# Attention block on one core: two query blocks start on the first 512 keys under a bound of their own, engines take turns on a PSUM bank, and the last output sums are held behind the last PV

## The chip, the cores and the metric

The kernel runs on one core of a Trainium2 chip. The metric is the device time of one execution in microseconds (us), the median of several runs. TensorE is called PE, VectorE DVE, ScalarE ACT, GpSimd POOL and SyncE SP. PSUM is where this kernel puts PE's products (tiles PA, PD and PO), in banks of 128 x 512 f32 values. "Span" is the time from the first to the last instruction of a profiled execution; it is some 1.8 us shorter than the time of the same run.

## The reference

```python
# x: 1 x 2048 x 448, wqkv: 448 x 1344, wo: 448 x 448, all bf16; H = 16 heads of 28
qkv = (x @ wqkv).reshape(B, S, 3, H, Dh).transpose(2, 0, 3, 1, 4)
q, k, v = qkv[0], qkv[1], qkv[2]
scores = jnp.einsum("bhqd,bhkd->bhqk", q, k) * (Dh ** -0.5)
p = softmax(scores, axis=-1)
o = jnp.einsum("bhqk,bhkd->bhqd", p, v)
out = o.transpose(0, 2, 1, 3).reshape(B, S, D) @ wo
```

## The kernel before

The 16 heads form four groups of four; a head is padded from 28 to 32 rows. A window is one group and one block of 512 queries; there are 16. In a window, each of 16 key tiles (128 keys) and four heads gives a score tile of 128 keys x 512 queries: 1024 tiles in all. Most tiles get their exponential on ACT, two at a time; the others go over DVE in three passes with a POOL product between them. PV products (exponentials times values) add a window's tiles up in one PSUM bank (PO).

```python
# two score tiles at once on ACT
nc.scalar.activation(out=PTA[pslot.idx][:, 0:len(ns) * QW], in_=PA[s.idx][:, 0:len(ns) * QW],
                     func=ACT.Exp, bias=ACT_BIAS, scale=ACT_SCALE)
# one score tile over DVE and POOL: p1, p2 (DVE), gq (POOL), f (DVE)
p1 = add(Op("DVE", P1, lambda: nc.vector.tensor_scalar(out=DU[b][:], in0=lo, ...)))
p2 = add(Op("DVE", P1, lambda: nc.vector.scalar_tensor_tensor(out=DV[b][:], in0=lo, ...)))
gq = add(Op("POOL", PTT, lambda: nc.gpsimd.tensor_tensor(out=DG[b][:], in0=DV[b][:], in1=DU[b][:], op=ALU.mult), ...))
f  = add(Op("DVE", P1, lambda: nc.vector.scalar_tensor_tensor(out=PTD[...], in0=PX[slot.idx][:], in1=DG[b][:], ...)))
```

The softmax subtracts a bound instead of the row's true maximum. The absolute values of a head's queries and its largest absolute keys, with a margin, are extra rows of the score product. The keys' maximum runs over all 2048 keys, so the first score of a group needs all four key blocks:

```python
# task_K: one of four key blocks of a group
red = add(Op("DVE", 0.61, lambda: nc.vector.tensor_reduce(
    out=KPART[g][:, sc:sc + 1], in_=ap(), axis=AX.X, op=ALU.max, apply_absolute_value=True), ...))
evs = [add(Op("ACT", 0.585, lambda pr=pr: nc.scalar.activation(      # waits for red; both read this bank
    out=KB[0][pr][:, cs], in_=ap(), func=ACT.Identity, bias=onescol[:, 0:1], scale=1.0), deps=[ops[-1], red], ...)) ...]
# task_kmax: over the four blocks, then written or broadcast into the keys' extra rows
m = add(Op("DVE", 0.12, lambda: nc.vector.tensor_reduce(out=KMAX[g][:], in_=KPART[g][:], axis=AX.X, op=ALU.max),
           deps=kmaxop[g], ...))
```

The order of the instructions on each engine is fixed when the kernel is built. The kernel lists operations with estimated durations, priorities and conditions, and a list scheduler in the kernel puts them in order; constants such as `QPR` or `UO` steer it. In the traces read here each engine works through its own list in that order: in the run below in which nine output sums stand ahead of the last PV products in PE's list, PE starts these sums at 402.07 us and those products at 403.88. In the last window, nine output products of the three earlier groups (`late_sums`, kind "A") may be placed before or after the last PV products; the final normalisation on DVE starts once PV has ended (in the trace of this kernel the last PV products start at 405.61 and take 0.39, DVE starts at 406.04):

```python
prev = add(Op("PE", 0.19, lambda: nc.tensor.matmul(out=PD[late_acc[tq]][:, 0:D],
    lhsT=OT[gg][NQC - 1][:, tq * P:(tq + 1) * P], rhs=WO[:, gg, :], start=(gg == 0), stop=False),
    prio=ACCP + tq + 0.1 * gg, kind="A", ...))
...
norm_dve(PO[:], DT[:], DR[:], ...)        # transpose, reciprocal, two transposes, two products, then four last matmuls
```

## Time and profile before

| | before |
|---|---|
| time, median of three runs (range) | 414.73 (414.67 to 415.01) |
| span of the profiled run | 413.1 |
| head: start to first exp | 16.38 |
| row: first exp to start of the last exp | 387.90, with 424 exps of 1024 columns |
| tail: start of the last exp to the end | 8.83 |

An "exp" is always one ACT instruction over two score tiles. A "step" is the time from the start of one to the start of the next; the steps were read from the starts in the trace. Their median is 0.916 us, and the mean of those without a hole is 0.9135. The kernel has six steps over 0.98; one is the second exp's (1.254), and four of the others are 1.17 to 1.19.

### The profile page before, as it was taken

The page shows a single profiled execution, that of the slowest core. Times are in us where ns is not written, and L with a number is a line of the kernel's source. Part 1 is how long each engine was busy: PE and PEld are TensorE (multiplying, and loading weights), DVE is VectorE, ACT ScalarE, POOL GpSimd, SP SyncE. Part 2 cuts the span into 40 slices and gives each one's busy share as a digit, 9 for nine tenths or more (in the row PEclk, how much of TensorE's full clock was granted, in tenths as well). Part 3 has the DMA queues.
Part 4 walks back from the last instruction along what each step waited for, and adds up shares of the span by engine and source line. Part 5 has one row for each costly group of instructions (what it writes and reads, how often), then busy time and mean ns, then how long its engine had stood idle before and what let it go on. Part 6 is the DMA issues. An engine that isn't in the chain of part 4 may idle for free.

```text
span 413.1 us, 7525 instructions
## 1 busy us (share of the span) xinstructions
PE 362.4 (88%) x2605; PEld 121.4 (29%) x2617; DVE 394.0 (95%) x696; ACT 400.0 (97%) x439; POOL 224.1 (54%) x203
## 2 busy tenths in 40 slices
PE   8988989898898889888898988979898888989995
PEld 4533232223232232322223222222322222222231
DVE  6899999999999999999999999999999999999975
ACT  4999999999999999999999999999999999999994
POOL 2155456464655556475465656547375656556450
PEclk9999999999999999999999999999999999999999
DMA  8410011202201001110400001010310101001012
GB/s 256 77 20 21 3 47 11 53 25 54 72 1 44 2 28 30 20 38 8 111 8 27 21 9 40 2 36 11 77 48 2 47 2 35 12 27 47 4 69 89
DMA packets 33413, 15.83 MB, mean 38 GB/s; under 512 B 26016, under 2 KB 30304, under 8 KB 33376
## 3 DMA queue, kind: packets, MB, share of 16 engines
q1 hardware_dynamic: 32304, 15.05, 14.5%
q8 instruction: 20, 0.33, 0.4%
q10 hardware_dynamic: 1072, 0.32, 0.3%
q14 instruction: 17, 0.14, 0.1%
HBM read 7.37 MB, written 1.96 MB: 23 GB/s over the span
## 4 chain that ended last, share of the span: by engine, by line
ACT 86%; issue 8%; PE 2%; DMA 2%; DVE 1%; SPq 0%; DVEq 0%; ACTq 0%
ACT PTA_131 L903 5%; ACT PTA_132 L903 4%; ACT PTA_133 L903 4%; ACT PTA_136 L903 4%; ACT PTA_135 L903 4%; ACT PTA_134 L903 4%; ACT PTA_145 L903 4%; ACT PTA_140 L903 4%; ACT PTA_139 L903 4%; ACT PTA_138 L903 4%; ACT PTA_137 L903 4%; ACT PTA_144 L903 4%; ACT PTA_142 L903 3%; ACT PTA_143 L903 3%; ACT PTA_141 L903 3%
## 5 line engine op out<-in xcount | busy, mean ns | idle before, releaser
L714 POOL TENSOR_TENSOR DG_181<-DV_175,DU_169 128x512 f16<-128x512 f16 x30 | 34.6, 1155 | 34.8 <-DVE DV_175 L711 34.6
L714 POOL TENSOR_TENSOR DG_182<-DV_176,DU_170 128x512 f16<-128x512 f16 x30 | 34.6, 1155 | 28.8 <-DVE DV_176 L711 28.7
L714 POOL TENSOR_TENSOR DG_184<-DV_178,DU_172 128x512 f16<-128x512 f16 x29 | 33.5, 1155 | 29.5 <-DVE DV_178 L711 28.2
L714 POOL TENSOR_TENSOR DG_186<-DV_180,DU_174 128x512 f16<-128x512 f16 x29 | 33.5, 1155 | 26.9 <-DVE DV_180 L711 26.7
L714 POOL TENSOR_TENSOR DG_185<-DV_179,DU_173 128x512 f16<-128x512 f16 x29 | 33.5, 1155 | 25.7 <-DVE DV_179 L711 25.6
L714 POOL TENSOR_TENSOR DG_183<-DV_177,DU_171 128x512 f16<-128x512 f16 x29 | 33.5, 1156 | 22.9 <-DVE DV_177 L711 22.7
L631 PEld LDWEIGHTS <-KB_1_94 64*128 64x128 bf16 x256 | 20.8, 92 | 48.4 <-issue 47.4
L631 PEld LDWEIGHTS <-KB_0_91 64*128 64x128 bf16 x256 | 20.5, 92 | 45.8 <-issue 42.1
L631 PEld LDWEIGHTS <-KB_1_92 64*128 64x128 bf16 x256 | 20.1, 93 | 45.8 <-issue 44.0
L631 PEld LDWEIGHTS <-KB_0_93 64*128 64x128 bf16 x256 | 20.3, 92 | 43.5 <-issue 42.5
L903 ACT ACTIVATE PTA_140<-PA_199 128x1024 bf16<-128x1024 f32 x18 | 22.4, 1247 | 0.0
L903 ACT ACTIVATE PTA_144<-PA_199 128x1024 bf16<-128x1024 f32 x18 | 22.4, 1245 | 0.0
L903 ACT ACTIVATE PTA_143<-PA_198 128x1024 bf16<-128x1024 f32 x18 | 22.3, 1241 | 0.0
L903 ACT ACTIVATE PTA_142<-PA_199 128x1024 bf16<-128x1024 f32 x18 | 22.3, 1239 | 0.0
L903 ACT ACTIVATE PTA_141<-PA_198 128x1024 bf16<-128x1024 f32 x18 | 22.3, 1236 | 0.0
L903 ACT ACTIVATE PTA_139<-PA_198 128x1024 bf16<-128x1024 f32 x17 | 21.1, 1241 | 0.0
L708 DVE TENSOR_SCALAR DU_171<-PD_202 128x512 f16<-128x512 uint16 x29 | 19.8, 682 | 1.0 <-PE PD_202 L631 0.7
L708 DVE TENSOR_SCALAR DU_172<-PD_200 128x512 f16<-128x512 uint16 x29 | 19.7, 681 | 0.9 <-PE PD_200 L631 0.9
L711 DVE SCALAR_TENSOR_TENSOR DV_178<-PD_200,DU_172 128x512 f16<-128x512 uint16 x29 | 19.8, 684 | 0.3
L711 DVE SCALAR_TENSOR_TENSOR DV_176<-PD_201,DU_170 128x512 f16<-128x512 uint16 x29 | 19.8, 683 | 0.2
L708 DVE TENSOR_SCALAR DU_169<-PD_200 128x512 f16<-128x512 uint16 x29 | 19.8, 682 | 0.2 <-PE PD_200 L631 0.2
L903 ACT ACTIVATE PTA_145<-PA_198 128x1024 bf16<-128x1024 f32 x16 | 20.0, 1247 | 0.0
(596 smaller groups left out, 1511.3 us busy)
## 6 DMA issues: line engine op xcount, KB each, us to landing
RRB_194<-SCR_196 SPq DMA_DIRECT2D x8, 256.0 KB
RRB_195<-SCR_197 SPq DMA_DIRECT2D x7, 256.0 KB
KB_1_94<-KB_0_93 SPq DMA_DIRECT2D x4, 128.0 KB
XS_127<-in_x_dram SPq DMA_DIRECT2D x1, 448.0 KB
XS_128<-in_x_dram SPq DMA_DIRECT2D x1, 448.0 KB
XS_129<-in_x_dram SPq DMA_DIRECT2D x1, 448.0 KB
XS_130<-in_x_dram SPq DMA_DIRECT2D x1, 448.0 KB
out_dram<-XS_127 SPq DMA_DIRECT2D x1, 448.0 KB
```

Source lines behind the costliest of these rows:

```text
L631: nc.tensor.matmul(out=ap, lhsT=KB[g % 2][i // 2][a:a + 64, j * P:(j + 1) * P], rhs=QB[w % NQB][i // 2][a:a + 64, :], start=True, stop=Tru ...
L708: p1 = add(Op("DVE", P1, lambda: nc.vector.tensor_scalar(out=DU[b][:], in0=lo, scalar1=SIG / 65536, scalar2=SIG * (SS - 0.5), op0=ALU.mult ...
L711: p2 = add(Op("DVE", P1, lambda: nc.vector.scalar_tensor_tensor(out=DV[b][:], in0=lo, scalar=65536 * (SS - 0.5 + CE / C3), in1=DU[b][:], o ...
L714: gq = add(Op("POOL", PTT, lambda: nc.gpsimd.tensor_tensor(out=DG[b][:], in0=DV[b][:], in1=DU[b][:], op=ALU.mult), deps=[p2], prio=n, kind ...
L903: nc.scalar.activation(out=PTA[pslot.idx][:, 0:len(ns) * QW], in_=PA[s.idx][:, 0:len(ns) * QW], func=ACT.Exp, bias=ACT_BIAS, scale=ACT_SCALE)
```

## The change

The intent is to start ACT's row earlier. Query blocks 0 and 1 of the first group take keys 0 to 511 (16 tiles each) under the maximum of these keys alone, which needs only the first block of x. Their partial PV sums are copied out of PO. Once the whole bound is known, a factor per query and head rescales them, and the rest of the block is added. Parts that go with it:

- the query weights are loaded second on the queue of the x blocks, and padded by ACT instead of POOL;
- the fourth block of x comes already transposed, by a DMA, not over PE and PSUM;
- reduce and copy of a key block's PSUM bank take turns as planned (in the kernel before, ACT's key copy waited twice for the reduce, 0.21 and 0.25 us), and DVE makes the copies of the second to fourth key block, which ACT made;
- the last output sums are held back while PV products are ready;
- many constants of the order are changed.

```diff
+    FB = TPC                # 4 key tiles = 512 keys
+    NF = 2                  # query blocks that start under their own bound
-    UO = 40
+    UO = 20
... (other constants cut)
     for b in range(NQC):
-        nc.sync.dma_start(out=XS[b][:], in_=x_perm[:, b * TPC:(b + 1) * TPC, :])
-    for (W, off) in ((WK, D), (WQ, 0)):
-        nc.scalar.dma_start(out=W[:, :, 0:GW], in_=wq3[:, :, off:off + GW])
+        if b < NQC - 1:
+            nc.sync.dma_start(out=XS[b][:], in_=x_perm[:, b * TPC:(b + 1) * TPC, :])
...
+        if b == 0:
+            nc.sync.dma_start(out=WQ[:, :, 0:GW], in_=wq3[:, :, 0:GW])
...
+    if XBAR:
+        for cc in range(CC):
+            nc.sync.dma_start(out=XT[NQC - 1][cc // 2][:, cc % 2, :],
+                              in_=bass.AP(x.tensor, x.offset + cc * CK, [[D, QW], [1, P]]), transpose=True)
...
+                evs[0].acq = lambda t: red.start is None or red.done(t)      # turns on one bank
+                red.acq = lambda t: evs[0].start is None or evs[0].done(t)
...
-                and kmrep[(g, j // TPC, i)].done(t))
+                and (w < NF and j < FB or kmrep[(g, j // TPC, i)].done(t)))
...
+    def task_factor(w):     # eight small matmuls, then
+        e = add(Op("ACT", 0.49, lambda: nc.scalar.activation(out=RRB[w][:], in_=bank(task)[:], func=ACT.Exp, scale=ACT_SCALE), ...))
+    def finish_block(w):
+        ev = add(Op("DVE", 0.62, lambda: nc.vector.tensor_copy(out=OSB[w][:], in_=PO[:]), ...))
+        first_part[w] = [add(Op("POOL", 1.22, lambda: nc.gpsimd.tensor_tensor(out=OSB[w][:], in0=OSB[w][:], in1=RRB[w][:], op=ALU.mult), ...))]
...
-        o = take_static(t, lambda o: o.kind == "A" and fits(o.dur, "F") or ...)
+        o = take_static(t, lambda o: o.kind == "A" and fits(o.dur, "F") and (pv_next[0] >= NROW or not pv_ready(pv_next[0], t)) or ...)
```

## The prediction

> **What bounds the kernel now.** I read the page first (busy shares, the 40 slices, the chain that ended last), then cut the span at the first and the last exp, then read both ends instruction by instruction.
>
> ```profile
> PE 362.4 (88%) x2605; PEld 121.4 (29%) x2617; DVE 394.0 (95%) x696; ACT 400.0 (97%) x439; POOL 224.1 (54%) x203
> ACT  4999999999999999999999999999999999999994
> ACT 86%; issue 8%; PE 2%; DMA 2%; DVE 1%; SPq 0%; DVEq 0%; ACTq 0%
> ```
>
> ACT is busy in every slice but the first and the last, and the chain runs along it for 86% of the span. The windows view (from:to, length, then busy us and count of PE, weight loads, DVE, ACT and POOL, granted clock, DMA share, GB/s) is cut at the start of the first and of the last exp:
>
> ```profile
> 0.00:16.38 16.38, 14.54 (x104) 7.92 (x106) 11.14 (x35) 9.62 (x13) 2.83 (x12) 1.00 0.69 180
> 16.38:404.28 387.90, 344.14 (x2488) 112.39 (x2497) 378.21 (x653) 387.67 (x424) 221.23 (x191) 1.00 0.13 31
> 404.28:413.10 8.82, 3.75 (x20) 1.09 (x16) 4.63 (x10) 2.68 (x5) 0.00 (x0) 0.91 0.29 104
> ```
>
> In the middle ACT works 387.67 of 387.90 us. So the kernel is three terms: a head of 16.38, a row of exps without holes, a tail of 8.82. The row has 424 exps of two score tiles each: 848 of the 1024 tiles; the other 176 go over DVE and POOL. From the start of the second exp (17.63) to that of the last (404.28) are 422 steps in 386.65 us, 0.916 a step. Only three things can move the time: when the first exp starts, what ACT must do until the last one, and holes.
>
> The head, from the chain in order of time (start, length, what):
>
> ```profile
> 1.63 6.31 DMA XS_129<-in_x_dram
> ...
> 10.19 0.61 PE PA_199 L311 x8
> 10.79 0.87 PE PD_202 L380 x4
> 11.66 0.86 PE PO L380 x4
> 12.52 0.88 PE PA_199 L380 x4
> ...
> 13.49 0.70 DVE KPART_95 L385
> ...
> 14.21 0.17 DVE KMAX_99 L410
> ```
>
> The first score needs the key bound over all 2048 keys, so four blocks of x must land, be transposed (L311), multiplied by the key weights (L380) and reduced (L385, L410) before it. ACT then:
>
> ```profile
> 14.29 0.69 ACT L474 ACTIVATE QB_0_85<-PD_201,offscol 128x512 bf16<-128x512 f32 x1 [0.24 <-PE PD_201 L466]
> ...
> 16.38 1.02 ACT L903 ACTIVATE PTA_131<-PA_198 128x1024 bf16<-128x1024 f32 x1 [0.25 <-PE PA_198 L631]
> 17.63 1.02 ACT L903 ACTIVATE PTA_132<-PA_199 128x1024 bf16<-128x1024 f32 x1 [0.23 <-PE PA_199 L631]
> ```
>
> The second exp starts 1.25 after the first, not 0.92, because the bounds of the other two heads come late: 0.33 lost.
>
> [...] the key copy on ACT waited twice for the reduce (KPART_95), 0.5 us together. [...] For the queue used here the trace shows: the broadcast of the bound to the last head began at about 19.55 and its score waited until 21.78, 2.2 us.
>
> **The change part by part.** Counts are from the order of instructions of the built kernel, durations from the trace.
>
> 1. The head. Query blocks 0 and 1 take keys 0 to 511 (16 score tiles each) under the bound of these keys alone, so the first score needs only the first block of x. Step by step:
> - The first block lands at 4.73, as before. The query weights now lie second on its queue (98 KB, in small packets). The x blocks land about 1.62 apart for 448 KB, which would be 0.35 for 98 KB[...].
> - ACT pads them (448 elements; 448-wide copies step by 0.43 in the tail): 6.2. Half of the second transposed half follows on ACT, the other on DVE: 6.75.
> - The last two key matmuls end 0.65 later, 7.4 to 7.5; reduce 0.69: 8.15; a clamp and a reciprocal on one column, about 0.15 each: 8.4.
> - Three query matmuls at 0.215 end near 8.1; ACT copies the queries (0.69): 8.8. DVE: absolute value 0.28, copy 0.2, two multiplies at 0.35: 10.0.
> - PE meanwhile transposes blocks 1 and 2, 32 in all at 0.06; the third block, now behind the query weights, lands at some 8.5 to 9. PE is free for the first score near 10.0, and that plus 0.46 (15.92 to 16.38 before) would be 10.5.
> - But ACT has, in its order, query copy (8.1 to 8.7), key copy for heads 0 and 2, which takes its turn after the reduce (to 9.35), a transposed half (0.92, to 10.25), key copy for heads 1 and 3 (0.65). First exp: 10.9 to 11.1. I take 11.0, so 5.4 saved.
> - Second exp: its bounds on DVE come after one transposed half (10.0 + 0.69 + 0.7 = 11.4), its score at 11.9, when the first exp ends. At most 0.1 lost, so 0.2 gained on the 0.33.
>
> 2. ACT's row. 425 exps instead of 424, as DVE takes 174 tiles instead of 176: +0.92. Two new exps of 512 columns, the factors that rescale the early part; 0.43 x 512/448 = 0.49 each: +0.98. Together +1.9.
>
> 3. DVE. Two tiles fewer at three passes of about 0.6: -3.6. Added: two partial sums out of the PV bank (0.6 each), the multiplies, copies and the wider key copies at the start, some 4. DVE is not on the chain in the middle and has about 9.7 us idle there; nothing lands on the end.
>
> 4. Holes in the early row. The first 32 tiles give ACT 15 exps (DVE takes two), to 11.0 + 15 x 0.92 = 24.8. By then keys 512 to 1023 must have been moved and the whole bound broadcast. DVE's order up to the bound is two transposed halves, three reduces, three key copies, one query copy and its multiplies: from 11.5 some 8.3 us, 19.9. Four broadcasts at 0.65 a piece on the queue, 2 us more: 23 to 24.6. Just in time; I allow 0.4. The fourth block of x comes transposed by DMA, and PE, which works in order, meets it before the seventh score pair, which must be out by about 16. It stands behind the third block (8.75) and 392 KB of value weights (1.4 at the rate of the blocks): 10.2; its own 512 KB at that rate is 1.85: 12. [...] I allow 0.4.
>
> 5. The tail. The nine early output matmuls move behind the last PV. Before, three of them stood among the scores at 399.5 and six behind the last PV, and DVE's normalisation (406.04 to 408.49) hid those. Nine at 0.19 end 1.9 after the last PV, and DVE still needs 2.2 before its first product. Nothing gained, nothing lost: 8.8 stays.
>
> Sum: -5.4 - 0.2 + 1.9 + 0.8 + 0 = -2.9; 414.7 - 2.9 = 411.8, and since the allowances for holes are on the careful side I put **411.6**.
>
> **The rivals.** (a) The DMA transpose is late. Each us past 16 is a us of ACT idle, since every later score stands behind that matmul. For it: the queues carried 182 GB/s between 4.7 and 16.4, so it competes; against it: some 4 us of slack. Landing at 19 would make 414.5. (b) The key moves and broadcasts are late. Twelve moves and four broadcasts on one issuing queue take about 10 us of issuing (0.6 each in the trace) where before six did; if broadcasts land at 27, 413.5. (c) DVE becomes the bound, having nearly no idle time from 11 to 40: score tiles keep their PSUM banks longer and PE stalls in order. Its 97% in the middle speaks for it, that it never held ACT up before against; +1 to +2. (d) The other way: the weights land by 5.2 and there are no holes: 410.0. (e) A gain over 2% would need 8.3 us; the whole shortening of the head is 5.4, and nothing else shrinks, so it can hardly be.
>
> **Range and chances.** The head is good to about 0.8, the holes run from 0 to 3, the rest is counted. That makes 409.8 to 413.8 for 8 in 10. Faster by over 2% (below 406.4): 0.02. Slower by over 2% (above 423.0): 0.02, which needs a stall that I have not seen. Within 2%: 0.96.
>
> **What would show it.** In the windows view of the changed kernel the first exp starts at 10.9 to 11.3; the steps stay 0.916; 425 wide exps and two narrow ones near 0.5 lie between it and the last, which starts near 401; the end comes 8.8 later. Between 11 and 30 ACT's waits show holes, on PE's scores, and PE's on the transposed fourth block or the broadcast bound: more than 2 us there and rivals (a) or (b) hold; holes later, on PSUM banks that DVE frees, are (c). A first exp after 12 would say that the weights' landing was mis-sized, and a tail shorter than 8.5 that moving the output matmuls did gain.

Passages are cut from the recorded text, at the marks, where it told of the hardware what no trace or run of this case shows. No term of the sum is cut: it came to -5.4 - 0.2 + 1.9 + 0.8 + 0 = -2.9, so 411.8, put as 411.6. What is cut lies inside two terms. In the head, an allowance for the landing of the query weights: the 6.2 of the next step counts from 5.75, which was the author's estimate, where the rate of the x blocks alone gives 4.73 + 0.35 = 5.08. In the holes, the reason for the second 0.4: a later landing of the transposed block. That a DMA which transposes moves at the rate of the blocks was not measured. The step of 0.916 and the 2.2 us from the start of a broadcast to the score that waits for it are from the trace.

## The result

The changed kernel takes 411.89 us (411.78 to 411.99, four runs) against 414.87 in the same rounds (414.67 to 415.01, four runs). The ratio is 0.9927, with a 95% interval of 0.9913 to 0.9941: within 2%, and truly less than 1. Every ratio here is the mean time of one kernel's runs over the mean of the other's runs of the same rounds, so it is not quite the ratio of the medians. The result is correct.

From the page of the changed kernel, the busy times, ACT's row of the 40 slices and the chain that ended last:

```profile
PE 362.4 (88%) x2613; PEld 120.9 (29%) x2613; DVE 395.4 (96%) x701; ACT 397.6 (97%) x437; POOL 225.6 (55%) x217
ACT  4999999999999999999999999999999999999993
ACT 83%; PE 8%; issue 7%; DVE 1%; ACTq 0%
```

ACT still bounds the kernel. Its busy time fell by 2.4 us: in the head it has 7 instructions and 5.25 us where it had 13 and 9.62, because copies of keys, of transposed halves and of queries moved to DVE or went away, and the row gained some 2. The windows view of the changed kernel, cut at the first and the last exp as for the kernel before (columns: stretch, length, busy us and count of PE, weight loads, DVE, ACT, POOL; clock; DMA share; GB/s):

```profile
0.00:11.20 11.20, 9.64 (x67) 5.80 (x68) 7.74 (x29) 5.25 (x7) 3.92 (x26) 1.00 1.00 207
11.20:401.05 389.85, 348.27 (x2509) 113.35 (x2509) 383.05 (x664) 389.73 (x428) 221.70 (x191) 1.00 0.14 33
401.05:410.13 9.08, 4.54 (x39) 1.71 (x37) 4.58 (x10) 2.67 (x5) 0.00 (x0) 0.95 0.28 101
```

| term | before | changed | difference | predicted |
|---|---|---|---|---|
| head | 16.38 | 11.20 | -5.17 | -5.4 |
| row | 387.90 | 389.85 | +1.95 | -0.2 + 1.9 + 0.8 |
| tail | 8.83 | 9.08 | +0.25 | 0 |
| span | 413.11 | 410.13 | -2.98 | -2.9 |

In the head, ACT's timeline of the changed kernel (start, length, what; in brackets the idle time before it and what ended that):

```profile
5.21 0.56 ACT L341 COPY WQP<-WQ 112x448 bf16<-112x448 bf16 x1 [2.74 <-DMA WQ<-in_wqkv_dram]
6.15 0.59 ACT L389 COPY XT<-PD 112x512 bf16<-112x512 bf16 x1 [0.37 <-PE PD L376]
8.39 0.69 ACT L620 ACTIVATE QB<-PD,offscol 128x512 bf16<-128x512 f32 x1 [1.66 <-PE PD L606]
8.97 0.77 ACT L492 ACTIVATE KB<-PD,bndcol,selcol 128x512 bf16<-128x512 f32 x1
9.64 1.01 ACT L389 COPY XT<-PA 112x1024 bf16<-112x1024 bf16 x1
10.53 0.80 ACT L492 ACTIVATE KB<-PD,bndcol,selcol 128x512 bf16<-128x512 f32 x1
11.20 4.97 ACT L1121 ACTIVATE PTA<-PA 128x1024 bf16<-128x1024 f32 x5
```

From 8.39 on ACT works without a gap: query copy, key copy, a transposed half, key copy, first exp. The exp at 11.20 stands behind ACT's own list; its score was on PE from 10.60. In the row, the two factors are the narrow exps of ACT:

```profile
34.14 0.85 ACT L860 ACTIVATE RRB<-PD 128x512 f32<-128x512 f32 x1
38.29 0.86 ACT L860 ACTIVATE RRB<-PO 128x512 f32<-128x512 f32 x1
```

The step from exp to exp across them is 1.382 and 1.394 us, so each takes 0.47 more than an ordinary step. Row by parts: one exp more, +0.91; two factors, 1.382 + 1.394 - 2 x 0.9136 = +0.95; the second exp's loss, 1.157 instead of 1.254, -0.10; all other steps, +0.2. That is 1.96 for a measured 1.95. Between 12.4 and 33.2 us no step is over 0.98.

### The profile page after: what moved, and what is told of

It reads as the page before. It is cut to its first block, busy times and chain, and to the rows that moved or that the text cites. A ratio compares the mean times of both kernels' runs of the same rounds, so it can differ in the third digit from the quotient of the medians.

```text
span 410.1 us, 7564 instructions
## 1 busy us (share of the span) xinstructions
PE 362.4 (88%) x2613; PEld 120.9 (29%) x2613; DVE 395.4 (96%) x701; ACT 397.6 (97%) x437; POOL 225.6 (55%) x217
## 3 DMA queue, kind: packets, MB, share of 16 engines
HBM read 6.91 MB, written 1.96 MB: 22 GB/s over the span
## 4 chain that ended last, share of the span: by engine, by line
ACT 83%; PE 8%; issue 7%; DVE 1%; ACTq 0%
ACT PTA L1121 83%; PE PA L808 3%; PE PO L977 1%; PE PA L355 1%; PE PO L677 0%; ACT RRB L860 0%; PE PD L476 0%; PE PD L376 0%; PE PD L606 0%; PE PD L808 0%; ACT OUTF L1250 0%; PE PO L606 0%; PE PO L476 0%; PE PD L758 0%; DVE DEN L824 0%
## 5 line engine op out<-in xcount | busy, mean ns | idle before, releaser
L1121 ACT ACTIVATE PTA<-PA 128x1024 bf16<-128x1024 f32 x425 | 390.8, 1245 | 0.1
L925 POOL TENSOR_TENSOR DG<-DV,DU 128x512 f16<-128x512 f16 x174 | 200.7, 1155 | 166.1 <-DVE DV L922 156.8
L808 PE MATMUL PA<-QB,KB 64*128 64x512 bf16 x850 | 167.0, 379 | 40.3 <-ACT PTA L1121 38.1
L808 PEld LDWEIGHTS <-KB 64*128 64x128 bf16 x1024 | 66.9, 92 | 185.8 <-issue 177.4
L919 DVE TENSOR_SCALAR DU<-PD 128x512 f16<-128x512 uint16 x174 | 117.4, 679 | 2.7 <-PE PD L808 2.3
L922 DVE SCALAR_TENSOR_TENSOR DV<-PD,DU 128x512 f16<-128x512 uint16 x174 | 117.9, 681 | 1.3
L938 DVE SCALAR_TENSOR_TENSOR PTD<-PD,DG 128x512 uint16<-128x512 f32 x174 | 117.8, 677 | 0.2 <-POOL DG L925 0.2
L977 PE MATMUL PO<-PTA,VA 128*32 128x512 bf16 x850 | 84.9, 386 | 0.0
L808 PE MATMUL PD<-QB,KB 64*128 64x512 bf16 x174 | 64.7, 376 | 1.1 <-DVE PTD L938 0.6
L977 PE MATMUL PO<-PTD,VA 128*32 128x512 bf16 x174 | 60.0, 386 | 0.0
L511 DVE TENSOR_SCALAR KB<-PO,onescol 128x512 bf16<-128x512 f32 x12 | 8.9, 740 | 0.0
L758 PE MATMUL PO<-WO,OT 128*128 128x448 bf16 x28 | 8.2, 358 | 0.0
```

Source lines behind the costliest of these rows:

```text
L808: nc.tensor.matmul(out=ap, lhsT=KB[g % 2][i // 2][a:a + 64, j * P:(j + 1) * P], rhs=QB[w % NQB][i // 2][a:a + 64, :], start=True, stop=Tru ...
L938: f = add(Op("DVE", P1, lambda: nc.vector.scalar_tensor_tensor(out=PTD[st["s"].idx][:].bitcast(U16), in0=PX[slot.idx][:], scalar=EBITS + C ...
L977: nc.tensor.matmul(out=PO[HP * st:HP * (st + 1), :], lhsT=VA[g][:, j, st, :], rhs=r["p"][i][1](), start=first, stop=last, tile_position=(0 ...
```

## The experiments

Twelve kernels ran, four, four, three and one to a call, each beside runs of the kernel before. In those calls the kernel before took 414.80, 414.71, 414.76 and 414.88; the changed kernel is compared by its 411.89 and by traces. The turns on a PSUM bank, the copies moved to DVE and the padding by ACT were not tried by themselves.

### Was it the bound of 512 keys that shortened the head?

**The changed kernel with the scores put behind the whole maximum.**

```diff
-    QPR = 50
+    QPR = 100
-                and (w < NF and j < FB or kmrep[(g, j // TPC, i)].done(t)))
+                and kmax_op[0].done(t) and (w < NF and j < FB or kmrep[(g, j // TPC, i)].done(t)))
```

> The changed kernel, but no score may be issued before the maximum over all 2048 keys exists, as in the kernel before; early blocks keep their partial sums and factors (one priority of the order, that of the query products, is doubled so that the order still fits). Theory (the head's gain comes from the bound of 512 keys alone, not from the earlier query weights, the rearranged loads or the narrower start): the whole bound is made at 19.3 to 20 us in the changed kernel, so the first exp falls at 19.8 to 20.5, 8.6 to 9.3 later than 11.2, and the time is 419.5 to 421. Rival (most of the gain comes from the loads and their order): DVE, ACT and PE then reach the whole bound sooner, the first exp comes by 14 or 15 and the time stays at 413 to 416.

Measured: 420.34 (420.23 to 420.43), ratio 1.0135 (1.0118 to 1.0152), correct. ACT's timeline of this kernel:

```profile
19.08 3.77 ACT L1121 ACTIVATE PTA<-PA 128x1024 bf16<-128x1024 f32 x4 [7.65 <-PE PA L808]
```

The first exp falls at 19.08 instead of 11.20, 7.9 later; the row is 0.3 shorter and the tail 0.9 longer (the cause of that is the tail trap told below: one product of an earlier block stands among the last sums). The theory holds: in this order the rearranged loads alone gain nothing. The first exp is even later than in the old order (16.38): DVE, which now also makes copies that ACT made, gets to the whole maximum only at 19.11. (The rule acts on the order: the score's place on PE is behind the work for the maximum. No data dependency was added. PE multiplies zeros from 15.00 to 18.71, and its first score, at 18.65, comes even before the maximum, so a real wait would have been a little longer still. An order made anew for the whole bound with these loads was not tried.)

**The kernel before with only the query weights moved.**

```diff
     for b in range(NQC):
         nc.sync.dma_start(out=XS[b][:], in_=x_perm[:, b * TPC:(b + 1) * TPC, :])
-    for (W, off) in ((WK, D), (WQ, 0)):
-        nc.scalar.dma_start(out=W[:, :, 0:GW], in_=wq3[:, :, off:off + GW])
+        if b == 0:
+            nc.sync.dma_start(out=WQ[:, :, 0:GW], in_=wq3[:, :, 0:GW])
+    nc.scalar.dma_start(out=WK[:, :, 0:GW], in_=wq3[:, :, D:D + GW])
```

> The kernel before with one edit: the query weights are loaded second on the queue of the x blocks, as in the changed kernel. Theory (the earlier query weights help only where the bound is made from the first block; in the old order they merely push x blocks 2 to 4 back by 0.5 to 0.8 us, and the bound waits for the fourth): 414.8 to 415.6. Rival (the query weights were what the head waited for, so moving them is the gain): 410 to 413.

Measured: 415.42 (414.96 to 416.25), ratio 1.0019 (1.0004 to 1.0034). PE's timeline of this kernel:

```profile
7.48 0.65 PE L312 MATMUL PD<-ident,XS 128*112 128x128 bf16 x8 [1.83 <-DMA XS<-in_x_dram]
```

The second block of x is transposed from 7.48 on instead of 6.35, and the first exp falls at 17.29 instead of 16.38. The four runs fall into two pairs, 414.96 and 415.00, 415.83 and 416.25; the profile is of the third, and the faster pair lies within the range of the kernel before in that call (414.49 to 415.06). So the early query weights gain nothing here and cost in some runs; the next run shows that they pay together with the narrow bound.

**The changed kernel with the query weights late again.**

```diff
+    nc.scalar.dma_start(out=WQ[:, :, 0:GW], in_=wq3[:, :, 0:GW])     # behind the key weights
-        if b == 0:
-            nc.sync.dma_start(out=WQ[:, :, 0:GW], in_=wq3[:, :, 0:GW])
-    WQLAT = 5.9
+    WQLAT = 8.7
```

> The query weights go back behind the key weights on ACT's queue, where they landed at 8.75 before; the plan is told so. Theory: they were on the path of the first score. Pad to 9.3, four products to 10.4, copy to 11.1, absolute value, copy and two bounds to 12.4, score and first exp at 12.9 to 13.5: 1.7 to 2.3 later than 11.2, 413.4 to 414.2 us. Rival: the transposes of the next blocks and ACT's copies set the first exp, the weights had slack: first exp by 11.7, 412.0 to 412.4 us.

Measured: 415.75 (413.94 to 416.23), ratio 1.0013 (0.9990 to 1.0036), correct. PE's timeline of the profiled run:

```profile
6.88 1.16 PE L475 MATMUL PD<-XT,WKP 112*128 112x512 bf16 x4
10.15 1.49 PE L605 MATMUL PD<-XT,WQP 112*128 112x512 bf16 x4 [2.12 <-ACT WQP L340]
11.43 1.06 PE L375 MATMUL PA<-ident,XS 128*112 128x128 bf16 x8
13.99 0.62 PE L375 MATMUL PD<-ident,XS 128*112 128x128 bf16 x8
```

The cost went in the expected direction but further: the first exp falls at 15.01, 3.8 later. PE stood idle for 2.12 us until the weights were padded. The four products after that took 1.49 us, where four in the run above took 1.03, and the transposes from 11.43 to 13.9 start 0.107 apart, against 0.056 from 14.0 on; the mean granted clock of this run is 0.995. So the wait on PE was followed by a second cost. Of four runs, the one with the highest mean clock (0.998) took 413.94, the other three (clock 0.992 to 0.995) 415.73 to 416.23. That fits such a slow stretch in some runs only; as just one run has a profile, this is not shown for the others.

### Are two early blocks needed?

**The changed kernel with one early block.**

```diff
-    NF = 2
+    NF = 1
-    QPR = 50
+    QPR = 100
-    Q2E = 40
-    Q2U = 70
+    Q2E = 20
+    Q2U = 30
+    open_when(d_slots[2], [xt_half[2]])
```

> Only query block 0 takes the first 512 keys under their own bound (the plan's limits for the second query block are moved forward with it, so that its queries are ready). Theory: the two blocks exist to give ACT work while the whole bound is made and broadcast. One block is 16 tiles, 8 exps, from 11.2 to 18.5; the bound on DVE, 20.05 in the changed kernel, comes up to 2.8 us earlier without the second block's queries, and four broadcasts of 0.65 plus 2 us follow: a hole on ACT of 3 to 6 us from 18.5 on, one narrow exp less (-0.5), so 414.5 to 417.5 us, ratio to before about 1.00 to 1.007. Rival: the bound has slack of its own and the second block buys nothing: hole under 1 us, 411 to 412 us.

Measured: 419.08 (418.84 to 419.19), ratio 1.0101 (1.0086 to 1.0116), correct. ACT's timeline, then DVE's at the end:

```profile
11.20 7.68 ACT L1122 ACTIVATE PTA<-PA 128x1024 bf16<-128x1024 f32 x8
23.70 2.86 ACT L1122 ACTIVATE PTA<-PA 128x1024 bf16<-128x1024 f32 x3 [4.82 <-PE PA L809]
```

```profile
407.75 2.22 DVE L763 TENSOR_TENSOR XS<-PD,KB 128x448 bf16<-128x448 f32 x4 [4.41 <-PE PD L759]
409.89 0.71 DVE L821 STREAM_TRANSPOSE DT<-PO 128x512 f32<-128x512 f32 x1
```

One block feeds ACT with eight exps, to 18.9, and then the rest of the keys' bound is missing: a hole of 5.0 us. The second block's exps fill this time. That part is as expected. The tail (11.65) is not: in this order four sums of an earlier output block (L763) stand on DVE before the final transpose (L821), and wait for PE products that the order put late. These 2.6 us belong to the order, not to the bound. I call this the tail trap; it returns below.

### What do the two factors cost?

Their steps show 0.95 us. Does the time fall by that much without them? Three kernels take parts of the cost away; all other orders stay.

**Without the factors.** A fill with 1.0 on POOL takes the place of each narrow exp; the result was still within the tolerance.

```diff
-        e = add(Op("ACT", 0.49, lambda: nc.scalar.activation(out=RRB[w][:], in_=bank(task)[:], func=ACT.Exp, scale=ACT_SCALE),
+        e = add(Op("ACT", 0.49, lambda: nc.gpsimd.memset(RRB[w][:], 1.0),
```

> Wrong result on purpose: the two narrow exps on ACT that make the rescaling factors are replaced by two fills on POOL at the same places; every other instruction on every engine keeps its order. Theory: ACT is what bounds the row, so both steps of 0.47 fall away whole: span -0.94, 410.9 to 411.1 us. Rival: the row is as tightly fed by DVE and PE, and what ACT saves comes back as holes before later exps: span -0.3 or less, 411.6 to 411.9 us.

Measured: 411.71 (411.46 to 411.99), ratio 0.9924 (0.9908 to 0.9941). PE's and ACT's timelines:

```profile
43.73 0.39 PE L808 MATMUL PA<-QB,KB 64*128 64x512 bf16 x2
44.75 0.39 PE L977 MATMUL PO<-PTA,VA 128*32 128x512 bf16 x2 [0.63 <-DVE KB L511]
```

```profile
46.10 2.86 ACT L1121 ACTIVATE PTA<-PA 128x1024 bf16<-128x1024 f32 x3 [0.59 <-PE PO L977]
```

ACT gained 0.95 at 33 and 37 us, but from the first to the last exp the row is only 0.25 shorter (389.60), so 0.70 was given back. Two steps hold it (0.79; the ordinary steps are 0.1 shorter in sum). One of 1.25 at 35.0 (0.33 over an ordinary one) lies where PE's list has value products and a single score between two score pairs, 1.25 us of work with no wait; this is read from the trace, and no run tried it. The other, at 44.4, is 1.68 where the changed kernel has 1.22, 0.46 more: PE could not start the PV products until DVE had copied a key block out of PO (L511), and the next scores and the next PV products stand behind these. The exp's wait ended with the latter, at 46.01; its own scores were done at 45.69.

**Without the factors and without the two DVE copies of the partial sums** (wrong: a fill with 0 on POOL).

```diff
-        ev = add(Op("DVE", 0.62, lambda: nc.vector.tensor_copy(out=OSB[w][:], in_=PO[:]), deps=[pvop], prio=-5000))
+        ev = add(Op("DVE", 0.62, lambda: (nc.gpsimd.memset(OSB[w][:], 0.0), None)[1], deps=[pvop], prio=-5000))
```

> The run without the two factor exps, and without the two DVE copies of the partial sums out of the PV bank as well (a fill on the idle POOL takes their place; wrong result on purpose). All other orders are the same. Theory (when ACT's two factors were taken away only 0.2 us of their 0.94 came back because DVE, with the copies, was as full as ACT just then): both together save 0.94 or more, 410.8 to 411.1. Rival (PE or a bank's turn holds the early row whatever DVE does): 411.5 to 411.8 as without the factors alone.

Measured: 411.85 (411.43 to 412.07), ratio 0.9929 (0.9915 to 0.9944). Nothing more was gained; the step at 44.5 is again 1.684. My theory, that the copies had filled DVE, failed. The trace says why: the copies lie before 33 us, and there DVE only waited longer for a query product (1.31 us instead of 0.79), which PE began at 33.98, and at 33.91 in the run before. From then on DVE was busy without a gap until 47.

**Without the factors and without two DVE instructions after that point** (wrong): the copy of the fourth block's values and one key reduction, replaced by fills on POOL.

```diff
+            if g == 0 and jq == 3:
+                nc.gpsimd.memset(o, 0.0)
+            elif eng == "ACT":
...
-            red = add(Op("DVE", RED, lambda: nc.vector.tensor_reduce(
+            red = add(Op("DVE", RED, lambda: nc.gpsimd.memset(KPART[g][:, sc:sc + 1], 1.0) if g == 1 and sc == 0 else nc.vector.tensor_reduce(
```

> The run without the two factor exps, and two DVE instructions that lie between 37 and 43 us replaced by fills on POOL: the copy of the fourth block's values (0.62) and one key reduction (0.69). Wrong result on purpose. Both earlier runs (factors away; factors and the copies of partial sums away) kept a step of 1.68 at 44.4 us, and there DVE was busy without a gap from 34.3 to 47 us, its start set by a query product that PE gave at 33.9 to 34.0. The copies of partial sums lay before that point, so their absence only lengthened DVE's wait for that product. Theory (DVE's unbroken row from 34.3 on sets when the PV bank comes free at 44.7): the key copy that ends at 44.7 now ends 1.2 to 1.3 earlier, the step at 44.4 shrinks from 1.68 to 0.92 to 1.1, and the time is 410.9 to 411.2. Rival (PE in order, or another bank, holds it): the step stays over 1.4 and the time at 411.5 to 411.8.

Measured: 411.12 (410.76 to 411.28), ratio 0.9912 (0.9898 to 0.9925). DVE's timeline without the factors alone, then in this kernel; after that PE's in this kernel:

```profile
43.95 0.74 DVE L511 TENSOR_SCALAR KB<-PO,onescol 128x512 bf16<-128x512 f32 x1
```

```profile
43.28 0.75 DVE L511 TENSOR_SCALAR KB<-PO,onescol 128x512 bf16<-128x512 f32 x1
```

```profile
44.06 0.39 PE L810 MATMUL PA<-QB,KB 64*128 64x512 bf16 x2 [0.33 <-ACT PTA L1123]
44.38 0.39 PE L979 MATMUL PO<-PTA,VA 128*32 128x512 bf16 x2
```

The key copy comes 0.67 earlier though this run's first exp was 0.34 later (11.48), PE waits for ACT again and no longer for DVE, and the step there is 1.05 instead of 1.68. From the first to the last exp the row now takes 388.93 us: 0.67 less than without the factors alone, and 0.92 less than in the changed kernel. (The step of 1.25 at 35 is still there; the step at 44 is now shorter than the changed kernel's, and the ordinary steps are shorter by 0.1 in sum, so that 0.92 is not simply the 0.95 of the factors.) So this is shown: around 44 us DVE holds the row as much as ACT does, and what ACT saves before it is gained only if DVE is relieved too, and after the point where its unbroken row begins.

### What do the held-back sums do?

```diff
-        o = take_static(t, lambda o: o.kind == "A" and fits(o.dur, "F") and (pv_next[0] >= NROW or not pv_ready(pv_next[0], t)) or ...)
+        o = take_static(t, lambda o: o.kind == "A" and fits(o.dur, "F") or ...)
```

> The rule that holds the nine early output products back until the last PV product is out is taken away; the order of ACT and DVE stays. What the prediction says: these products are hidden either way, so 411.7 to 412.1 us. Rival: in the new order they now stand together ahead of the last 18 or so PV products, PE works in order, and the last PV ends 9 x 0.19 = 1.7 us later: 413.4 to 413.8 us, of which the tail from the last exp takes all.

Measured: 413.95 (413.68 to 414.13), ratio 0.9977 (0.9962 to 0.9992), correct. PE's timeline of the changed kernel at the end, then of this kernel:

```profile
402.03 0.82 PE L977 MATMUL PO<-PTA,VA 128*32 128x512 bf16 x12
402.78 1.88 PE L841 MATMUL PD<-WO,OT 128*128 128x448 bf16 x9
405.08 0.55 PE L1245 MATMUL PD<-WO,OTL 128*128 128x448 bf16 x2 [0.42 <-DVE OTL L1243]
```

```profile
402.07 1.88 PE L841 MATMUL PD<-WO,OT 128*128 128x448 bf16 x9
404.11 0.82 PE L977 MATMUL PO<-PTA,VA 128*32 128x512 bf16 x12
407.16 0.55 PE L1245 MATMUL PD<-WO,OTL 128*128 128x448 bf16 x2 [2.23 <-DVE OTL L1243]
```

Without the rule the nine sums (1.88 us) stand before the last PV products, DVE's normalisation starts 404.98 - 401.21 = 3.77 after the last exp's start instead of 402.90 - 401.05 = 1.85, and the tail grows from 9.08 to 11.02. With the rule the sums run while DVE normalises: PE then waits 0.42 for DVE, so they are free. In the new order the rule is worth 1.9 to 2.1 us.

### What does the DMA transpose save?

Three kernels transpose the fourth block of x on PE again. The first:

```diff
-    XBAR = True
+    XBAR = False
-    BW = (-1, 2, 2)
+    BW = (-1, 2, 2, 0)
-    QPR = 50
+    QPR = 100
... (the shape of the tile XT cut)
```

> The changed kernel, but the fourth block of x is transposed on PE like the other three (16 small transposes and two copies out of PSUM on DVE or ACT), not by a DMA; one priority of the order doubled as in the run with the full bound. Theory (the DMA transpose takes 1.4 us of copies off a full DVE or ACT in the early row): the whole bound comes 1.4 to 2 us later, ACT gets a hole of 0.5 to 1.5 us near 25 us or two exps more, and the time is 413 to 415. Rival (the DMA transpose only moves work that had room): 411.6 to 412.3.

Measured: 415.15 (414.92 to 415.26), ratio 1.0010 (0.9995 to 1.0025), and the result was wrong. (Its tail, 9.77, has the tail trap as well.) The unused path has wrong release conditions: the transposes of the fourth block overwrote halves of the third in two PSUM banks before these had been copied out. In the next kernel they wait for the right copies:

```diff
-             ((PO[:], None), (PD[1][:], -2)), ((PD[2][:], 2), (PO[:], 3)))
+             ((PO[:], None), (PD[1][:], -2)), ((PD[2][:], 2), (PO[:], 4)))
-    k0_wait = [..., lambda: [xt_half[5]], lambda: [xt_half[4]]]
+    k0_wait = [..., lambda: [xt_half[5]], lambda: [xt_half[7]]]
-                acq = lambda t: xt_half[2].done(t)
+                acq = lambda t: xt_half[6].done(t)
```

> The run without the DMA transpose, mended: there the fourth block's transposes overwrote halves of the third block in two PSUM banks before these had been copied out (the release conditions of that unused path named the wrong copies), so its result was wrong. Now they wait for the right ones. Theory (the DMA transpose saves the full early row two copies and PE 16 transposes, and the plan two exps): correct, 414.5 to 416, with 427 exps (+1.8), and the rest in holes before 45 us and in a later maximum over all keys than 19.3 to 20. Rival (it moves work that had room): 411.6 to 412.3.

Measured: 419.66 (419.06 to 420.26), ratio 1.0114 (1.0099 to 1.0129), correct, but far over what was expected. Its order has two faults of its own: a step of 2.96 at 68.6 us, and the tail trap (tail 11.08). The comparison is not clean. So the constants of the order were searched again:

```diff
-    NTAIL = 12
+    NTAIL = 8
-    QPR = 50
+    QPR = 60
-    Q2E = 40
-    Q2U = 70
+    Q2E = 60
+    Q2U = 90
-    BW = (-1, 2, 2)
+    BW = (-1, 2, 2, 2)
-    EVP = (-1200, -4365, -900, 0)
+    EVP = (-1200, -4365, -900, -4000)
-    HENG = ('ACT', 'ACT', 'DVE', 'DVE')
+    HENG = ('ACT', 'ACT', 'DVE', 'ACT')
     (and the mended conditions above)
```

> The changed kernel without the DMA transpose once more, with the best order that a search over six constants gave (ACT takes one of the fourth block's two copies). The run mended before this one came out at 419.66, but its order fell into two traps of its own: a step of 2.96 at 68.6 us, and three output products of an earlier query block placed behind the last sums, which DVE waited for before its final normalisation (tail 11.08). This order has neither: nothing of an earlier block stands behind the last PV. Theory (the transpose by DMA takes two copies off the full early row): two more PSUM copies (0.69 on DVE, 0.92 on ACT) and one exp more in the row (426) cost 1.8 to 3, the tail stays 9.0 to 9.2, and the time is 413.5 to 415. Rival (it moves work that had room): 411.6 to 412.5.

Measured: 414.40 (414.24 to 414.60), ratio 0.9988 (0.9972 to 1.0005), correct. ACT's timeline:

```profile
13.07 1.01 ACT L389 COPY XT<-PO 112x1024 bf16<-112x1024 bf16 x1
68.12 2.85 ACT L1121 ACTIVATE PTA<-PA 128x1024 bf16<-128x1024 f32 x3 [0.87 <-PE PO L977]
```

The tail is 8.99 and the row 392.50, 2.65 over the changed kernel's. Of this, one exp more is 0.92 and the copy at 13.07 is 0.95 (the step across it is 1.862). The step at 66.0 is 2.09 where the changed kernel has a step of 1.18 near there: 0.91 more. The first two are the price of doing without the DMA transpose in this order; the third may belong to the order alone. So, against the best order found without it, the transpose by DMA is worth 1.9 to 2.5 us; as constants of the order differ too (the first exp comes at 10.97), this is not a clean price. My prediction took it as a risk only.

The four transpose DMAs also held the issuing queue: in the changed kernel from 3.15 to 10.98 us, 1.26 to 2.85 us each, where the five loads before them took 0.41 to 0.49 to issue. The four weight loads next on the queue were issued from 11.02 on, and the first move of the keys at 15.42.

### A try at a better version

Six constants of the order were changed, found by a search in the kernel's own scheduler; the work is the same.

```diff
-    NTAIL = 12
-    PARTD = 60
-    UO = 20
-    J1 = 8
-    FE = 40
-    KENG = ('ACT', 'DVE', 'DVE', 'DVE')
+    NTAIL = 8
+    PARTD = 40
+    UO = 30
+    J1 = 9
+    FE = 48
+    KENG = ('DVE', 'DVE', 'DVE', 'DVE')
```

> The changed kernel with six constants of its order changed (fewer score tiles on DVE close to the end, output work placed a little later, all early key copies on DVE); the work is the same. It is an attempt at a better version: if the last PV products stand in a shorter row at the end, the tail of 9.08 falls by 0.2 to 0.3 and the time is 411.6 to 411.8. Rival (what is left in tail and head is fixed by chains of single instructions): 411.8 to 412.3.

Measured: 413.43 (413.00 to 413.64), ratio 0.9967 (0.9955 to 0.9980), correct: 1.5 us slower than the changed kernel, and a miss for both theories. PE's and DVE's timelines at the end:

```profile
403.71 0.35 PE L758 MATMUL PD<-WO,OT 128*128 128x448 bf16 x1
```

```profile
404.10 0.62 DVE L762 TENSOR_TENSOR XS<-PD,KB 128x448 bf16<-128x448 f32 x1 [0.98 <-PE PD L758]
404.64 0.70 DVE L820 STREAM_TRANSPOSE DT<-PO 128x512 f32<-128x512 f32 x1
```

It is the tail trap. One output product of an earlier block (L758) stands among the sums on PE. DVE has that block's sum before its final transpose, so the normalisation starts 3.14 after the last exp's start (404.64 - 401.50) instead of 1.85. The tail is 10.35. Besides, the key copy moved to DVE delays the second exp: its step is 1.511 instead of 1.157. No version that beats the changed kernel was found.

## Why the prediction was right, point by point

**The time.** 411.6 was predicted and 411.89 measured. The head's gain and the growth of the row carry it, as the prediction said.

**Step 1, the head.** Shown by the run with the scores behind the whole maximum: the narrow bound is the cause. The instant of the first exp was put at 11.0 and came at 11.20; the list of ACT that the prediction named is the one in the trace. Two sizes inside were off. The query weights were padded from 5.21 on, not 5.75 (the allowance above): rival (d) was right in this one part. Nothing came of it, because ACT then waited 1.66 for the query products. PE made the sixteen transposes of the first block, from 4.63 to 6.33, at 0.107 each and the later ones at 0.056, so the key products ended at 7.70 and not at 7.4 to 7.5. This varies from profile to profile: in the kernel before with the early query weights all sixteen, from 4.59 on, took 1.06 us, 0.056 each; in the kernel before the first eight took 0.73 and the next eight 0.056 each. The first exp came at 11.34 with the sums back and at 11.48 without the two DVE instructions, in the same order up to there. A miss of 0.2 is within that. The second exp lost 0.24 and not 0.1.

**Step 2, ACT's row.** 425 exps and two factors were counted as +1.9; they make +0.91 and +0.95, 1.86 together. The trace agrees. What the prediction didn't see is that these 0.95 cannot be had back by freeing ACT alone.

**Step 3, DVE.** "Nothing lands on the end" was right for the changed kernel. But rival (c) was nearer than it was given credit for: from 34 to 47 us DVE runs without a gap, and when ACT was freed by 0.95, only 0.25 came back; 0.46 was lost to a wait for DVE at 44 us and 0.33 to PE's list at 35.

**Step 4, the holes.** 0.8 was allowed and 0.2 came: this is the term of the sum that was mis-sized most. The fourth block was on PE at 15.85 with no wait. The bound's broadcasts were issued from 20.59 on, and the first score that needs one came at 24.47, after 0.20 of idle time that the trace puts down to ACT. Rivals (a) and (b), late transposes and late broadcasts, didn't happen. Rival (d) had both of its conditions nearly right, weights by 5.2 and no early holes, but not its 410.0. That the two blocks were needed to cover that time is shown by the run with one: 5.0 us of hole.

**Step 5, the tail.** 0 was predicted and +0.25 came. The row of 24 PV products at the end ends some 0.1 later after the last exp than in the kernel before, and what follows takes another 0.16; neither was tried by itself. "Nothing gained" holds against the old order. But in the new order the rule is needed: without it the same sums cost 1.9 to 2.1.

**The sum.** The allowance that was too large in step 4 (0.6) and the sizes that were too favourable in steps 1 and 5 (0.2 in the head, 0.1 in the second exp, 0.25 in the tail) offset each other. The sum of the terms, 411.8, came within 0.1 of the measured time partly for that reason, which is luck; the mechanism was right, and the sizes were right to some 0.6.

## What to carry to other kernels

In this kernel one engine's row of equal work sets the time (ACT is busy for 97% of the span), and the start of that row is a term by itself: narrowing what the first item needs (here, a maximum over 512 keys, mended later by a factor) brought 5.17 us, where taking both factors out of the row brought 0.25. It needs early work that lasts until the wide result arrives: with one block instead of two a hole of 5.0 us came. Removing an operation from the bounding engine gained here only as much as the next engine left free just there: of ACT's 0.95, 0.25 came back, no more with DVE relieved before 33 us, and 0.92 with DVE relieved after 34. So find where that engine's unbroken row begins, and relieve it after that point, not before. In a fixed order, look at what stands on an engine before its last chain: one late small product of an older block, waited for in order, lengthened the tail by 0.7 to 2.6 us in five kernels here.
